# Pooled attention ahead of two gated MLPs: the attention rebuilt around two score products and a maximum inside the product

## The chip, the cores and the metric

The program runs on one NeuronCore of a Trainium2 chip. The metric is device time of one execution in microseconds (us); times of the same kernel agree within about 0.3%.

## The reference

```python
# q, k, v: 2 batches x 8 heads x 1152 tokens x 64, float32
q_pool = q.reshape(B, H, S // 2, 2, D).mean(axis=3)          # 576 pooled queries
scores = (1 / sqrt(D)) * q_pool @ k.transpose(0, 1, 3, 2)     # 576 x 1152 a head
scores = scores - max(scores, axis=-1)
attn = exp(scores); attn = attn / (sum(attn, axis=-1) + 1e-9)
x = (attn @ v) -> 1152 tokens x 512
h = relu(x @ w_in) ** 2;  y = h @ w_out                       # 512 -> 2048 -> 512
out = ((y @ w_a) * (y @ w_b)) @ w_out2                        # 512 -> 1536 -> 512
```

The weights arrive as float64 words; the chip makes float32 of them. A float32 operand x is split into hi, which is x rounded to float32r (12 significant bits), and lo = x - hi; a product is hi*hi + hi*lo + lo*hi.

## The kernel before

Work is done head by head in three stages: the attention (16 heads), then `mlp1`, then `mlp2`; the two MLPs take their products from `split_mm` (L488 to L490). Instructions run on each engine in the order in which the program issues them (a manual schedule). TensorE (PE) is followed in two rows, matmuls and weight loads (PEld).

In the attention a head has two units, each one half of its 576 queries: 288 columns. The steps of a unit u:

- `trans` (L285, L293) transposes [hi | lo] of k and of the pooled q, so that the 128 partitions hold 64 hi and 64 lo features. `kT` is [k_hi; k_lo], `qB` is [q_hi; q_lo], `qC` is the same with its halves exchanged.
- `scores` (L321, L322): for each of the 9 key tiles `kT` is the stationary side, and `qB`, then `qC` move past it, so that all four parts of the product are added up. ScalarE (ACT) copies the result from PSUM to SBUF (L247). Keys lie on partitions, queries along the columns.
- `colmax` (L333): VectorE (DVE) takes the maximum over the 9 key tiles, and GpSimd (POOL) takes it over the 128 partitions with `partition_all_reduce` (L338), result in `gm`.
- `sub` (L342): DVE subtracts `gm`, three key tiles at a time; `expo` (L346): ACT takes the exponential in place.
- `values` (L355): v, with a block of ones beside it for the denominators, is the stationary side; the float32 exponentials, not split, move past it, 9 products of 288 columns.
- `denom`, `recip`, `scale`, `x_hi`, `x_lo` divide by the denominators and write the split result to `xh`, `xl`, which the first MLP reads.

The START table writes out the order of the first units; from then on a fixed pattern of slots has the scores of a unit four slots ahead of its values. POOL also does the splits of k and q (L261, L265, L274), two small transfers for `qC` (L304, L305) and parts of the end. In the last four slots the first four MLP tiles (`early_mm`, `early_post`) and their weights (`w_step`) are worked in.

Of the kernel before, what the change touches and what calls it, by code (L numbers as in the profile page):

```python
# [23 lines left out]
k_hi 0 1 A; q_sum 0 0 V; k_hi 0 0 V; k_hi 0 2 V; k_lo 0 0 P; q_hi 0 0 A; q_lo 0 0 V; q_sum 0 1 V; q_hi 0 1 A  # L24
k_lo 0 1 V; k_lo 0 2 P; trans 0 3 o AAA; q_lo 0 1 P; k_hi 1 * V; trans 0 0 t V; trans 0 1 o A
trans 0 4 o VAV; q_sum 1 * V; q_hi 1 * V; scores 0 0 A; load_q 2; k_lo 1 * P; scores 0 1 A; trans 1 2 o A
load_k 3; trans 0 2 o V; scores 0 2 A; load_k 2; load_v 2; scores 2 0 A; trans 1 1 t A; colmax 0 0
q_lo 1 * P; scores 0 3 A; scores 0 4 A; trans 1 0 t A; load_q 3; q_sum 2 * P; colmax 0 1; trans 1 3 o AVV
q_sum 3 * P; q_hi 2 * V; scores 2 1 A; scores 2 2 A; load_v 3; k_hi 3 * A; scores 2 3 A; k_lo 3 * P
k_hi 2 * V; q_lo 2 * V; load_q 4; trans 1 4 o AAV; k_lo 2 * P; scores 1 0 A; scores 2 4 A; trans 2 4 o AAA  # L30
sub 0 0; scores 1 1 A; scores 3 0 A; load_v 0; colmax 2; trans 2 3 o AAV; w_load 3; load_k 4; scores 1 2 A
trans 3 0 o A; q_hi 3 * V; scores 1 3 A; load_k 5; trans 3 2 o A; q_lo 3 * P; trans 2 2 t A; scores 3 1 A
sub 0 1; q_sum 4 * P; trans 2 0 o V; scores 1 4 A; expo 0 0; scores 3 2 A; sub 0 2; load_q 5; scores 4 0 A
trans 3 1 t A; expo 0 1; values 0 0; colmax 1; sub 2 0; scores 3 3 A; scores 3 4 A; trans 2 1 t A; expo 0 2
trans 3 3 o VVV; values 0 1; trans 3 4 o AAV; w_step 2; scores 4 1 A; values 0 2; k_hi 4 * A; sub 2 1
scores 4 2 A; values 0 3; k_lo 4 * P; expo 2 0; load_v 1; q_hi 4 * A; load_k 6; sub 2 2; values 0 4
q_lo 4 * P; colmax 3; sub 1 0; scores 5 0 A; sub 1 1; q_sum 5 * P; scores 4 3 A; expo 2 1; values 2 0
scores 5 1 A; expo 2 2; load_q 6; scores 5 2 A; values 2 1; scores 4 4 A; values 2 2; denom 0; scores 5 3 A
expo 1 0; scores 5 4 A; k_hi 5 * A; sub 1 2; values 2 3; values 2 4; w_step 2
"""  # L40
START_SLOT = 2


@with_exitstack
def kernel(
# [646 lines left out]
```

## Time and profile before

| | |
|---|---|
| time, median of 2 runs | 985.65 us (985.35 to 985.96) |
| the profiled execution: span | 983.4 us (which of the two times is its own is not listed; the median lies 2.25 us above the span) |
| PE matmuls busy | 729.4 us, 74% |
| DVE busy | 557.4 us, 57% |
| ACT busy | 419.5 us, 43% |
| POOL busy | 151.7 us, 15% |

The span is from the first to the last instruction. A row of a group gives the instructions of one source line with their mean length, then the idle time of their engine just before them and what ended it; "issue" there is time in which the engine waited for nothing that the profile shows. [...] Matmuls are pipelined: what one costs is read from the distance between the starts of two, not from its own length.

### The profile page before, as it was taken

The page shows a single profiled execution, that of the slowest core. Times are in us where ns is not written, and L with a number is a line of the kernel's source. Part 1 is how long each engine was busy: PE and PEld are TensorE (multiplying, and loading weights), DVE is VectorE, ACT ScalarE, POOL GpSimd, SP SyncE. Part 2 cuts the span into 40 slices and gives each one's busy share as a digit, 9 for nine tenths or more (in the row PEclk, how much of TensorE's full clock was granted, in tenths as well). Part 3 has the DMA queues.
Part 4 walks back from the last instruction along what each step waited for, and adds up shares of the span by engine and source line. Part 5 has one row for each costly group of instructions (what it writes and reads, how often), then busy time and mean ns, then how long its engine had stood idle before and what let it go on. Part 6 is the DMA issues. An engine that isn't in the chain of part 4 may idle for free. (4 is left out here: it accounts for less than half of the span.)

```text
span 983.4 us, 10073 instructions
## 1 busy us (share of the span) xinstructions
PE 729.4 (74%) x3830; PEld 659.7 (67%) x3830; DVE 557.4 (57%) x657; ACT 419.5 (43%) x769; POOL 151.7 (15%) x151
## 2 busy tenths in 40 slices
PE   6372757446366366357446899999999999999998
PEld 5362545335345255246335799999999999899987
DVE  7546474544635445455556789349756677127721
ACT  6353535345345344345332656237523454225510
POOL 3211322123123122123111222000000000000000
PEclk9696777867767767778677899999999999999999
DMA  5210502102003003001000122223213333103212
GB/s 151 83 48 1 115 24 49 24 25 58 14 24 73 0 25 72 1 12 37 0 1 0 43 86 87 87 84 108 68 62 105 110 128 117 57 22 116 77 33 65
DMA packets 57905, 56.36 MB, mean 57 GB/s; under 512 B 21024, under 2 KB 50400, under 8 KB 57856
## 3 DMA queue, kind: packets, MB, share of 16 engines
q1 hardware_dynamic: 55712, 51.88, 18.5%
q0 software_dynamic: 1920, 3.54, 1.7%
q8 instruction: 30, 0.49, 0.2%
q10 hardware_dynamic: 224, 0.30, 0.1%
q14 instruction: 19, 0.16, 0.0%
HBM read 49.81 MB, written 2.36 MB: 53 GB/s over the span
## 5 line engine op out<-in xcount | busy, mean ns | idle before, releaser
L333 DVE TENSOR_REDUCE mx<-s 128x288 f32<-128x2592 f32 (+1 forms) x32 | 146.8, 4587 | 235.0 <-POOL gm L338 234.7
L355 PE MATMUL o<-s,v 128*128 128x288 f32 x576 | 192.1, 463 | 8.2 <-ACT s L346 7.6
L321 PE MATMUL ps<-qB,kT 128*128 128x288 f32 x288 | 117.6, 419 | 100.9 <-ACT s L247 100.7
L321 PEld LDWEIGHTS ps<-qB,kT 128*128 128x128 f32 x288 | 63.9, 222 | 112.6 <-ACT s L247 107.6
L355 PEld LDWEIGHTS o<-s,v 128*128 128x128 f32 x576 | 118.2, 222 | 30.4 <-ACT s L346 8.3
L293 PE MATMUL pt<-idr,qhl 96*128 96x96 f32 x96 | 21.4, 348 | 105.6 <-POOL qhl L274 105.0
L346 ACT ACTIVATE s<-s 128x864 f32<-128x864 f32 x96 | 88.5, 924 | 25.1 <-DVE s L342 24.9
L342 DVE TENSOR_TENSOR s<-s,gm 128x864 f32<-128x864 f32 x96 | 96.3, 1057 | 2.6 <-POOL gm L338 2.6
L247 ACT COPY s<-ps 128x576 f32<-128x576 f32 (+1 forms) x160 | 91.6, 585 | 10.5 <-PE ps L322 8.1
L322 PE MATMUL ps<-qC,kT 128*128 128x288 f32 x288 | 92.5, 332 | 1.6 <-DVE qC L249 1.6
L293 PEld LDWEIGHTS pt<-idr,qhl 96*128 96x128 f32 x96 | 14.8, 182 | 116.1 <-POOL qhl L274 110.6
L168 DVE TENSOR_TENSOR wlo<-wx,whi 128x512 fp32r<-128x512 f32 x60 | 41.8, 696 | 54.6 <-ACT whi L134 54.5
L322 PEld LDWEIGHTS ps<-qC,kT 128*128 128x128 f32 x288 | 65.2, 226 | 6.1 <-DVE qC L249 1.8
L338 POOL PARTITION_ALL_REDUCE gm<-mx x32 | 38.5, 1202 | 191.9 <-issue 164.6
L134 ACT CAST whi<-wx 128x512 fp32r<-128x512 f32 x68 | 42.1, 620 | 55.9 <-DVE wx L153 55.8
L489 PE MATMUL y<-gl,whi 128*128 128x384 f32 x192 | 64.6, 337 | 1.2 <-DVE gl L479 1.2
L488 PE MATMUL y<-gh,whi 128*128 128x384 f32 x192 | 64.6, 336 | 0.0
L490 PE MATMUL y<-gh,wlo 128*128 128x384 f32 x192 | 64.6, 336 | 0.0
L247 ACT CAST qB<-pt 128x288 fp32r<-128x288 f32 x30 | 12.0, 401 | 117.2 <-PE pt L293 117.1
L490 PE MATMUL h<-xh,wlo 128*128 128x384 f32 (+1 forms) x176 | 57.6, 327 | 0.0
L488 PE MATMUL h<-xh,whi 128*128 128x384 f32 (+1 forms) x176 | 57.5, 327 | 0.0
L489 PE MATMUL h<-xl,whi 128*128 128x384 f32 (+1 forms) x176 | 57.5, 327 | 0.0
(92 smaller groups left out, 1590.2 us busy)
## 6 DMA issues: line engine op xcount, KB each, us to landing
raw<-in_moe_w_out_dram SPq DMA_DIRECT2D x28, 512.0 KB, 3.3
raw<-in_moe_w_in_dram SPq DMA_DIRECT2D x16, 512.0 KB, 3.8
raw<-in_moe_w_a_dram SPq DMA_DIRECT2D x12, 512.0 KB, 3.5
raw<-in_moe_w_b_dram SPq DMA_DIRECT2D x12, 512.0 KB, 3.5
v<-in_v_dram SPq DMA_DIRECT2D x16, 288.0 KB, 4.2
kin<-in_k_dram SPq DMA_DIRECT2D x15, 288.0 KB, 2.9
qin<-in_q_dram SPq DMA_DIRECT2D x15, 288.0 KB, 3.3
qC<-qB POOLq DMA_DIRECT2D x24, 144.0 KB, 4.3
```

Of the source, the lines that this page charges most:

```text
L134: nc.scalar.copy(w["hi"], w["x"].bitcast(F32))
L168: eng.tensor_tensor(out=lo, in0=x.bitcast(F32), in1=hi.bitcast(F32), op=ALU.subtract)
L247: nc.scalar.copy(out, in_)
L321: nc.tensor.matmul(pt[:, t - 2 * j, :CQ], w, qB[h][:, sl], start=True, stop=False)
L322: nc.tensor.matmul(pt[:, t - 2 * j, :CQ], w, qC[h][:, sl], start=False, stop=True)
L333: nc.vector.tensor_reduce(out=e, in_=st[u][:, kts].rearrange("p c q -> p q c"), op=ALU.max, axis=AX.X)
L342: nc.vector.tensor_tensor(out=s, in0=s, in1=g[:, None, :].to_broadcast([P, 3, CQ]), op=ALU.subtract)
L346: nc.scalar.activation(s[:, 3 * i:3 * i + 3, :], s[:, 3 * i:3 * i + 3, :], AF.Exp, scale=SCALE)
L355: nc.tensor.matmul(om[u][:, :CQ], w, st[u][:, t, :], start=t == 0, stop=t == KT - 1)
L488: nc.tensor.matmul(ps, lh, rh, start=i == 0, stop=False)
L489: nc.tensor.matmul(ps, lh, rl, start=False, stop=False)
L490: nc.tensor.matmul(ps, ll, rh, start=False, stop=i == n - 1)
```

## The change

A head is worked on whole, all 576 queries at once, and the scores are made twice.

First (`maxima`) with 116 queries as the stationary side and the keys moving: queries lie on partitions, so DVE's reduction along the columns (negated) gives each query's maximum over half of the keys; ten such pieces make a head, five groups of queries that start at the columns in `QO` (the last overlaps the one before by 4). `max_split` joins the halves, splits the negated maximum into hi and lo and puts both beside zeros into `mz`; `trans_max` transposes this, so that the negated maximum lies in rows D and D + 1 of `qb`, under the high part of q. `kb` holds the high part of k above rows of ones.

Second (`scores`): `k1` x `qa` and `kb` x `qb` in one accumulation; the rows of ones add the negated maximum, so PSUM holds scores with the maximum subtracted, and ACT takes the exponential straight from PSUM. `exp_hi` (ACT) and `exp_lo` (DVE) split it. In `values` the split exponentials are the stationary side, 116 queries each, and [v_lo | v_hi | 1 1] moves: 130 columns past the high part, 66 past the low one. The result has queries on partitions; `normal` scales it there, and `trans_x` transposes each pair of heads into `xh`, `xl`. Copies that cross partitions (`move`) are transfers on SyncE's (SP's) queue; splits of q, k and v go to POOL. The START table, the warm-up products, `colmax`, `sub`, `denom`, `recip`, `scale` are gone. PSUM has three shared two-bank tiles and one two-bank output tile. The MLPs are not changed; their weights are first requested in the last head.

```diff
-START = """
...
-START_SLOT = 2
...
+    TQ = 116
+    QO = [0, 116, 232, 348, 460]
+    NQ = len(QO)
+    VW = 2 * D + 2
...
-            ps_s = es.enter_context(tc.tile_pool(name="ps_s", bufs=2, space=PSUM))
-            ps_o = es.enter_context(tc.tile_pool(name="ps_o", bufs=3, space=PSUM))
-            ps_t = es.enter_context(tc.tile_pool(name="ps_t", bufs=1, space=PSUM))
...
+            ps_p = es.enter_context(tc.tile_pool(name="ps", bufs=3, space=PSUM))
+            po_p = es.enter_context(tc.tile_pool(name="po", bufs=1, space=PSUM))
...
+            k1 = [ap.tile([P, S], F32R, name=f"k1_{i}") for i in range(NB)]
+            kb = [ap.tile([P, S], F32R, name=f"kb_{i}") for i in range(NB)]
+            qa = [ap.tile([P, SQ], F32R, name=f"qa_{i}") for i in range(NB)]
+            vv = [ap.tile([P, KT, VW], F32R, name=f"vv_{i}") for i in range(NB)]
+            qb = [ap.tile([P, SQ], F32R, name=f"qb_{i}") for i in range(2)]
+            q0 = [pp.tile([P, SQ], F32R, name=f"q0_{i}") for i in range(2)]
+            mz = [pp.tile([TQ, NQ, P], F32R, name=f"mz_{i}") for i in range(2)]
...
+            def move(out, in_):
+                nc.sync.dma_start(out=out.bitcast(F32), in_=in_.bitcast(F32))
...
+                t = k1[h % NB]
+                sl = slice(6 * part * P, (6 * part + n) * P)
+                copy(e, t[:, sl].rearrange("p (b w) -> p b w", b=n // 3), ps[:, :n // 3, :3 * P].bitcast(F32))
+                move(kb[h % NB][:D, sl], t[:D, sl])
...
+                t = qa[h % NB]
+                copy(e, t.rearrange("p (b w) -> p b w", b=2), ps[:, :, :CQ].bitcast(F32))
+                move(q0[h % 2][:D], t[D:])
+                move(t[D:], t[:D])
...
+            def maxima(h, n):
+                i, half = divmod(n, 2)
+                if n == 0:
+                    mh[h] = ap.tile([TQ, NQ, 2], F32, tag="mh", bufs=2, name=f"mh{h}")
+                ps = ps_tile(f"pm{h}_{n}")
+                qs = slice(QO[i], QO[i] + TQ)
+                for c in range(2):
+                    ks = slice((2 * half + c) * CQ, (2 * half + c + 1) * CQ)
+                    nc.tensor.matmul(ps[:TQ, c, :CQ], qa[h % NB][:, qs], k1[h % NB][:, ks], start=True, stop=False)
+                    nc.tensor.matmul(ps[:TQ, c, :CQ], q0[h % 2][:, qs], kb[h % NB][:, ks], start=False, stop=True)
+                nc.vector.tensor_reduce(
+                    out=mh[h][:, i, half:half + 1], in_=ps[:TQ, :, :CQ], op=ALU.max, axis=AX.XY, negate=True
+                )
+            def max_split(h):
+                m = mh.pop(h)
+                z = mz[h % 2]
+                nm = ap.tile([TQ, NQ], F32, tag="nm", bufs=2, name=f"nm{h}")
+                nc.vector.tensor_tensor(out=nm, in0=m[:, :, 0], in1=m[:, :, 1], op=ALU.min)
+                nc.vector.tensor_copy(z[:, :, D], nm)
+                less("V", z[:, :, D + 1], nm, z[:, :, D])
+                move(qb[h % 2][:D], q0[h % 2][:D])
...
+            def trans_max(h, e="A"):
+                ps = ps_tile(f"px{h}", F32R)
+                for i in range(NQ):
+                    nc.tensor.matmul(
+                        ps[:, i // 4, (i % 4) * TQ:(i % 4 + 1) * TQ], mz[h % 2][:, i, :], idr[:TQ, :TQ],
+                        is_transpose=True, start=True, stop=True,
+                    )
+                for sl, src in by_tiles(ps):
+                    copy(e, qb[h % 2][D:, sl], src[D:].bitcast(F32))
...
+            def scores(h, t):
+                ps = ps_tile(f"ps{h}_{t}")
+                ks = slice(t * P, (t + 1) * P)
+                for c in range(2):
                     sl = slice(c * CQ, (c + 1) * CQ)
...
-                copy(e, st[u][:, 2 * j:2 * j + len(kts), :], pt[:, :len(kts), :CQ])
-
...
-                nc.vector.tensor_reduce(out=e, in_=st[u][:, kts].rearrange("p c q -> p q c"), op=ALU.max, axis=AX.X)
...
-                    nc.gpsimd.partition_all_reduce(g, m, P, bass.bass_isa.ReduceOp.max)
...
-            def sub(u, i):
-                s, g = st[u][:, 3 * i:3 * i + 3, :], mx_t[u]
-                nc.vector.tensor_tensor(out=s, in0=s, in1=g[:, None, :].to_broadcast([P, 3, CQ]), op=ALU.subtract)
-
-            def expo(u, i):
-                s = st[u]
-                nc.scalar.activation(s[:, 3 * i:3 * i + 3, :], s[:, 3 * i:3 * i + 3, :], AF.Exp, scale=SCALE)
...
-                    nc.tensor.matmul(om[u][:, :CQ], w, st[u][:, t, :], start=t == 0, stop=t == KT - 1)
...
+                    nc.tensor.matmul(ps[:, c, :CQ], k1[h % NB][:, ks], qa[h % NB][:, sl], start=True, stop=False)
+                    nc.tensor.matmul(ps[:, c, :CQ], kb[h % NB][:, ks], qb[h % 2][:, sl], start=False, stop=True)
+                e = ex[h, t] = ap.tile([P, SQ], F32, tag="ex", bufs=3, name=f"ex{h}_{t}")
+                nc.scalar.activation(e.rearrange("p (b w) -> p b w", b=2), ps[:, :, :CQ], AF.Exp, scale=SCALE)
...
+            def exp_hi(h, t):
+                eh[h, t] = ap.tile([P, SQ], F32R, tag="eh", bufs=4, name=f"eh{h}_{t}")
+                nc.scalar.copy(eh[h, t], ex[h, t])
...
+            def exp_lo(h, t, e="V"):
+                el[h, t] = ap.tile([P, SQ], F32R, tag="el", bufs=4, name=f"el{h}_{t}")
+                less(e, el[h, t], ex.pop((h, t)), eh[h, t])
...
+            def values(h, t):
+                if t == 0:
+                    ou[h] = po_p.tile([P, 2, 512], F32, tag="o", name=f"o{h}")
+                hi, lo = eh.pop((h, t)), el.pop((h, t))
+                for i in range(NQ):
+                    b, c0 = i // 3, (i % 3) * VW
+                    qs = slice(QO[i], QO[i] + TQ)
+                    o = ou[h][:TQ, b]
+                    nc.tensor.matmul(
+                        o[:, c0:c0 + VW], hi[:, qs], vv[h % NB][:, t, :],
+                        start=t == 0 and i % 3 == 0, stop=t == KT - 1, skip_group_check=True,
+                    )
+                    nc.tensor.matmul(
+                        o[:, c0 + D:c0 + VW], lo[:, qs], vv[h % NB][:, t, D:],
+                        start=False, stop=t == KT - 1, skip_group_check=True,
+                    )
...
+            def normal(h):
...
+                for sl, src in parts:
+                    nc.scalar.copy(ol[:, sl], src[:, :, :D])
+                for sl, src in parts:
+                    nc.vector.tensor_scalar(out=dn[:, sl], in0=src[:, :, 2 * D], scalar1=1e-9, scalar2=None, op0=ALU.add)
+                for sl, src in parts:
+                    nc.vector.tensor_tensor(out=ol[:, sl], in0=src[:, :, D:2 * D], in1=ol[:, sl], op=ALU.add)
+                nc.vector.reciprocal(dn, dn)
+                x = xt[h // 2][:, :, (h % 2) * D:(h % 2 + 1) * D]
+                nc.gpsimd.tensor_tensor(out=x, in0=ol, in1=dn[:, :, None].to_broadcast([TQ, NQ, D]), op=ALU.mult)
...
+            def trans_x(p):
...
+                for sl, src in by_tiles(ps):
+                    to = slice(b * SQ + sl.start, b * SQ + sl.stop)
+                    nc.scalar.copy(xh[:, pr, to], src)
+                    less("V", xl[:, pr, to], src, xh[:, pr, to])
...
+            split_q(0, "VAV")
+            split_k(0, "AV")
+            load(2)
+            trans_q(0)
+            trans_k(0, 0)
+            trans_k(0, 1)
...
+            for n in range(2 * NQ):
+                maxima(0, n)
+                if n == 2:
...
+            max_split(0)
...
+            trans_max(0)
+            MAXIMA = (2, 1, 1, 2, 1, 1, 2, 0, 0)
...
+            for h in range(NH + 1):
+                n = 0
+                for t in range(KT if h < NH else 2):
+                    if h < NH:
+                        scores(h, t)
+                        exp_hi(h, t)
+                    if h + 1 < NH:
+                        for _ in range(MAXIMA[t]):
+                            maxima(h + 1, n)
+                            n += 1
+                    if h < NH:
+                        exp_lo(h, t)
+                    g = h * KT + t - 2
+                    if g >= 0:
+                        values(*divmod(g, KT))
+                    if t == 1 and h:
+                        normal(h - 1)
...
+                    if h + 2 < NH:
+                        if t == 1:
+                            trans_k(h + 2, 0)
+                        if t == 2:
+                            trans_k(h + 2, 1)
+                        if t == 4:
+                            trans_q(h + 2)
+                    if t == 5 and h and h % 2 == 0:
+                        trans_x(h // 2 - 1)
+                    if h + 1 < NH:
+                        if t == 7:
+                            max_split(h + 1)
+                        if t == 8:
+                            trans_max(h + 1)
+                    if t == 2 and h + 3 < NH:
+                        split_k(h + 3)
+                    if t == 4 and h + 3 < NH:
+                        split_q(h + 3)
+                        load(h + 4)
+                    if t == 5 and h + 2 < NH:
+                        split_v(h + 2)
+                        load_v(h + 4)
+                    if h == NH - 1:
                         w_step(NE)
-                if s - 1 in do_t:
-                    load_v(do_t[s - 1])
-                if s == NU - 5:
-                    qk_stack.close()
+                        w_step(NE)
+                        if t in (2, 4, 6, 8):
+                            early_mm(ps_p, t // 2 - 1)
+                        if t in (3, 5, 7):
+                            early_post(gpool, t // 2 - 1)
+                if h == NH - 2:
+                    prep_stack.close()
                     gpool = gs.enter_context(tc.tile_pool(name="gpool", bufs=1, side="right", reuse_waits="tile"))
+            early_post(gpool, 3)
+            trans_x(NH // 2 - 1)
```

POOL, from the split of a head on, in the kernel before (`gm` is the maximum over partitions, `khl` and `qhl` the split k and q; an ISA row without tiles changes POOL's configuration):

```order
L338 ISA
L338 ISA gm_898<-mx_896 128x288
L261 ISA
L261 TENSOR_TENSOR khl_894<-kin_616,khl_894 128x9x64
L274 TENSOR_TENSOR qhl_923<-qin_619,qhl_923 96x6x64
L304 DMA qC_917<-qB_916 64x576
L305 DMA qC_917<-qB_916 64x576
L392 TENSOR_TENSOR xl<-xf_563,xh 128x288
L338 ISA
L338 ISA gm_988<-mx_986 128x288
```

And in the changed kernel, one whole head (`xt` the scaled output, `vv` the split v):

```order
L397 TENSOR_TENSOR xt_1272<-ol_1587,dn_1588 116x5x64
L237 CAST khl_1640<-kin_1403 128x9x64
L244 TENSOR_TENSOR khl_1640<-kin_1403,khl_1640 128x9x64
L251 TENSOR_TENSOR qin_1405<-qin_1405 96x6x64
L237 CAST qhl_1713<-qin_1405 96x6x64
L244 TENSOR_TENSOR qhl_1713<-qin_1405,qhl_1713 96x6x64
L237 CAST vv_108<-vin_1121 128x9x64
L244 TENSOR_TENSOR vv_108<-vin_1121,vv_108 128x9x64
```

The maximum and every change of configuration have left POOL; the casts of k, q and v and the low part of v have come to it.

PE in the middle of the attention before (`o` the output, `s` the exponentials, `v` values and ones):

```order
L321 MATMUL ps_0_2274<-qB_2112,kT_2111 128x288
L322 MATMUL ps_0_2274<-qC_2113,kT_2111 128x288
L321 MATMUL ps_0_2274<-qB_2112,kT_2111 128x288
L322 MATMUL ps_0_2274<-qC_2113,kT_2111 128x288
L355 MATMUL o_2280<-s_1981,v_92 128x288 x2
```

And one step of the changed kernel, a key tile t of a head: its scores (`ps`), a piece of the next head's maxima (`pm`), and the values (`o`) of the key tile two steps back, of whose five pairs of products two are shown:

```order
L347 MATMUL ps_4_3279<-qa_105,k_0_99 128x288
L348 MATMUL ps_4_3279<-qb_112,kb_102 128x288
L347 MATMUL ps_4_3279<-qa_105,k_0_99 128x288
L348 MATMUL ps_4_3279<-qb_112,kb_102 128x288
L310 MATMUL pm_6_3288<-k_1_100,qa_106 116x288
L311 MATMUL pm_6_3288<-kb_103,q_0_113 116x288
L310 MATMUL pm_6_3288<-k_1_100,qa_106 116x288
L311 MATMUL pm_6_3288<-kb_103,q_0_113 116x288
L368 MATMUL o_3226<-vv_108,eh_2_3216 116x130
L372 MATMUL o_3226<-vv_108,el_2_3224 116x66
L368 MATMUL o_3226<-vv_108,eh_2_3216 116x130
L372 MATMUL o_3226<-vv_108,el_2_3224 116x66
```

The value products have become ten narrow ones a key tile, and the products for the maxima stand between the scores and them.

PE of the changed kernel where one head's steps end and the next one's begin (`px` the transposed maxima, which ACT copies into `qb`):

```order
L368 MATMUL o_3226<-vv_108,eh_6_3362 116x130
L372 MATMUL o_3226<-vv_108,el_6_3376 116x66
L332 MATMUL px_3435<-idr,mz_115 128x116 x5
L347 MATMUL ps_0_3443<-qa_106,k_1_100 128x288
L348 MATMUL ps_0_3443<-qb_111,kb_103 128x288
```

The second product of the new head reads `qb`, which hangs on the transposition two rows above it.

## Rows read from the trace of the kernel before

**Rows 1.** The page: the span, busy time by engine, the granted clock in 40 slices.

```profile
span 983.4 us, 10073 instructions
...
PE 729.4 (74%) x3830; PEld 659.7 (67%) x3830; DVE 557.4 (57%) x657; ACT 419.5 (43%) x769; POOL 151.7 (15%) x151
...
PEclk9696777867767767778677899999999999999999
```

**Rows 2.** Stretches: busy us (instructions) of each engine, granted clock, DMA share, GB/s.

```profile
383.00:393.00 10.00, 9.63 (x55) 7.76 (x53) 7.17 (x4) 7.30 (x13) 2.30 (x3) 1.00 0.27 59
440.00:560.00 120.00, 71.61 (x320) 58.94 (x321) 72.15 (x53) 48.04 (x80) 22.10 (x23) 0.79 0.07 18
566.00:983.40 417.40, 411.88 (x2312) 399.36 (x2310) 246.90 (x446) 168.59 (x324) 13.63 (x10) 1.00 0.27 83
```

**Rows 3.** The page's costliest groups: busy us, mean ns, idle before them.

```profile
L333 DVE TENSOR_REDUCE mx<-s 128x288 f32<-128x2592 f32 (+1 forms) x32 | 146.8, 4587 | 235.0 <-POOL gm L338 234.7
...
L338 POOL PARTITION_ALL_REDUCE gm<-mx x32 | 38.5, 1202 | 191.9 <-issue 164.6
```

**Rows 4.** The line of the maximum over partitions: its instructions, min/median/max ns.

```profile
L338 POOLq MODIFY_POOL_CONFIG  x62: 1/4/49, 14.0 to 542.6; - x62
```

**Rows 5.** Timeline: start us, length us, instruction, idle before it and what ended it.

```profile
260.48 4.50 DVE L333 TENSOR_REDUCE mx<-s 128x288 f32<-128x2592 f32 x1 [8.04 <-POOL gm L338]
...
271.76 0.61 PE L321 MATMUL ps<-qB,kT 128*128 128x288 f32 x1 [14.73 <-ACT s L247]
...
276.76 4.57 DVE L333 TENSOR_REDUCE mx<-s 128x288 f32<-128x2592 f32 x1 [7.02 <-POOL gm L338]
```

**Rows 6.** Timeline of PE: products of 288 columns, and the f32 value products.

```profile
388.50 1.14 PE L355 MATMUL o<-s,v 128*128 128x288 f32 x4
389.25 0.51 PE L321 MATMUL ps<-qB,kT 128*128 128x288 f32 x1
389.60 0.29 PE L322 MATMUL ps<-qC,kT 128*128 128x288 f32 x1
...
565.98 0.30 PE L488 MATMUL h<-xh,whi 128*128 128x288 f32 x1
...
573.10 0.29 PE L488 MATMUL h<-xh,whi 128*128 128x288 f32 x1
```

**Rows 7.** Timeline of PE: transpositions, 288 columns at the low clock, 256 columns.

```profile
10.65 0.63 PE L285 MATMUL pt<-idr,khl 128*128 128x128 f32 x6
11.21 0.40 PE L321 MATMUL ps<-qB,kT 128*128 128x288 f32 x1
...
531.00 0.45 PE L488 MATMUL e<-xh,whi 128*128 128x288 f32 x1
531.24 0.45 PE L489 MATMUL e<-xl,whi 128*128 128x288 f32 x1
...
977.97 0.28 PE L489 MATMUL o<-wlo,th 128*128 128x256 f32 x1
978.09 0.28 PE L490 MATMUL o<-whi,tl 128*128 128x256 f32 x1
```

**Rows 8.** Groups by line, each shape apart: busy us, mean ns, idle before.

```profile
L247 ACT COPY s<-ps 128x576 f32<-128x576 f32 x128 | 79.4, 631 | 5.4 <-PE ps L322 3.3
...
L261 POOL TENSOR_TENSOR khl<-kin,khl 128x576 fp32r<-128x576 f32 x15 | 26.9, 1798 | 84.4 <-issue 77.4 <-ACT s L346 7.0
...
L247 ACT CAST khl<-kin 128x576 fp32r<-128x576 f32 x13 | 8.8, 675 | 0.1
...
L479 DVE TENSOR_TENSOR gl<-g,gh 128x576 fp32r<-128x576 f32 x4 | 3.5, 865 | 0.4
...
L333 DVE TENSOR_REDUCE mx_end<-s 128x288 f32<-128x864 f32 x1 | 1.1, 1130 | 0.0
```

**Rows 9.** The page's DMA issues: count, KB each, median us from issue to landing.

```profile
raw<-in_moe_w_in_dram SPq DMA_DIRECT2D x16, 512.0 KB, 3.8
...
qC<-qB POOLq DMA_DIRECT2D x24, 144.0 KB, 4.3
```

**Rows 10.** Timeline of PE: the first scores.

```profile
9.39 0.37 PE L321 MATMUL ps<-qB,kT 128*128 128x288 f32 x1 [0.24 <-DVE kT L249]
```

More of the change, by code (lines that the diff above doesn't have):

```diff
@@ L18 @@
 PSUM = bass.MemoryType.PSUM
-START = """
[L24 to L40, printed above, removed]
-START_SLOT = 2
 @with_exitstack
@@ L243, in attention @@
+            for i in range(2):
+                nc.gpsimd.memset(q0[i][D:].bitcast(F32), 0.0)
+                nc.gpsimd.memset(mz[i].bitcast(F32), 0.0)
             engines = {"A": nc.scalar, "V": nc.vector, "P": nc.gpsimd}
@@ L249, in copy @@
                     engines[e].tensor_copy(out, in_)
-            def part(c):
-                return slice(None) if c == "*" else slice(3 * int(c), 3 * int(c) + 3)
-            def k_hi(h, c="*", e="A"):
-                if h not in khl:
-                    khl[h] = qk.tile([P, KT, 2, D], F32R, tag="khl", bufs=2, name=f"khl{h}")
-                copy(e, khl[h][:, part(c), 0, :], kin[h][:, part(c)])
-            def k_lo(h, c="*", e="P"):
-                hi, lo = (khl[h][:, part(c), i, :] for i in range(2))
-                engines[e].tensor_tensor(out=lo, in0=kin[h][:, part(c)], in1=hi.bitcast(F32), op=ALU.subtract)
@@ L263, in q_sum @@
-            def q_sum(h, c="*", e="P"):
-                a, b = (qin[h][:, part(c), i, :] for i in range(2))
-                engines[e].tensor_tensor(out=a, in0=a, in1=b, op=ALU.add)
-            def q_hi(h, c="*", e="A"):
-                if h not in qhl:
-                    qhl[h] = qk.tile([QP, QT, 2, D], F32R, tag="qhl", bufs=2, name=f"qhl{h}")
-                copy(e, qhl[h][:, part(c), 0, :], qin[h][:, part(c), 0, :])
-            def q_lo(h, c="*", e="P"):
-                hi, lo = (qhl[h][:, part(c), i, :] for i in range(2))
-                engines[e].tensor_tensor(out=lo, in0=qin[h][:, part(c), 0, :], in1=hi.bitcast(F32), op=ALU.subtract)
@@ L398, in attention @@
-            load_k(1)
-            load_q(1)
-            warm = ps_t.tile([P, 512], F32R, tag="t", name="warm")
-            for i in range(NWARM):
-                nc.tensor.matmul(warm[:, :P], idr, idr, is_transpose=True, start=True, stop=True)
-            steps = dict(
-                load_k=load_k, load_q=load_q, load_v=load_v, k_hi=k_hi, k_lo=k_lo, q_sum=q_sum, q_hi=q_hi, q_lo=q_lo,
-                trans=trans, scores=scores, colmax=colmax, sub=sub, expo=expo, values=values, denom=denom,
-                w_load=w_load, w_step=w_step,
-            )
@@ L408, in attention @@
-            for step in START.replace("\n", ";").split(";"):
-                if step.strip():
-                    name, *args = step.split()
-                    steps[name](*(int(a) if a.isdigit() else a for a in args))
-            do_a, do_b, do_t = {}, {}, {}
-            for h in range(2, NH):
-                t = 4 * (h // 2) - 6 + h % 2 + (h < 4)
-                do_t[t], do_b[t - 1], do_a[t - 2] = h, h, h
-            seq = [0, 2, 1, 3] + list(range(4, NU))
-            def at_slot(f, p, *args, second=False):
-                if 0 <= p < NU and not (second and unit(seq[p])[2] == 0):
-                    f(seq[p], *args)
```

265 lines of the change are left out of this document (100 added, 165 removed).

## The prediction

> **What bounds the kernel now.** I read the page first: TensorE (PE) is 74% busy, but its slices fall into two stages, with half-idle digits and a granted clock of 0.6 to 0.8 up to slice 22, and 9s at full clock behind it [rows 1]. The stretches put the border in time: from 566.0 us, when the first product belonging to the MLP alone starts, PE is busy 411.9 of 417.4 us at clock 1.00, while 440 to 560 us shows 71.6 busy of 120 at 0.79 [rows 2]. The change touches the first stage; the 417.4 us behind it keep their instructions, and I carry them over whole.
>
> Inside the attention no engine is full, so the question is which wait ends last. The groups by line name it: VectorE (DVE) waits 234.7 us in front of its column maximum, all for `gm`, the maximum over partitions that GpSimd (POOL) makes [rows 3]. POOL's own idle time shows why: it sits before `gm` 164.6 us on "issue", that is, on nothing that the profile shows, and 77.4 us before the split of k [rows 3, 8]; 62 changes of the POOL configuration stand on the line of the maximum [rows 4]. The maximum itself takes 1.2 us; what costs is POOL's change between it and ordinary arithmetic, some 5 us each way (164.6 over 32 maxima, 77.4 over 15 splits). The timeline shows the beat: column maxima start at 260.48 and 276.76 us, one half-head (a unit) in 16.3 us, and the second comes behind 7.02 us of idle DVE [rows 5]. 32 such units make the 566 us.
>
> **The change, part by part.** Removed: all 32 partition maxima, their configuration changes, 96 subtractions on DVE and the plain-f32 value products. The listing of POOL's new order holds no configuration change between heads, so this bound goes entirely. What is late next is read by adding up each engine for one head (16 heads).
>
> PE. Products of 288 columns: from 565.98 to 573.10 us 54 of them start one behind the other at full clock, 0.132 us each [rows 6]; I take 0.133. Scores: 9 key tiles x 4 = 36, 4.8 us. Maxima: 10 x 4 = 40, 5.3 us. Values: 9 tiles x 5 query groups = 45 pairs, one product of 130 moving columns and one of 66, each with a new stationary of 116 columns. No row has a float32r product this narrow, so I bound it. Below: 288 columns cost 0.133 and 256 cost 0.12 [rows 6, 7], 0.41 ns a column; a pair is (130 + 66) x 0.41 = 0.08 us, and 0.11 with the 15 ns that each product has left over. Above: the f32 values of now, where four records and one product of 0.133 fill 388.50 to 389.60, so 0.24 a record; 576 records for 288 value products make two each, 0.48 us for 288 columns or 1.68 ns a column [rows 6]; a pair is then 0.33. The nearest row in width and type is the transposition of 128 float32r columns with a new 128-column stationary each: six in 0.56 us, 0.093 [rows 7]. I take 0.09 a product, 0.18 a pair, 8.1 us a head. [...] Transpositions: 9 for k, 6 for q, 5 for the maxima and half of 5 for the output (plain f32, taken double), 2.2 us. Sum for PE 20.4 us.
>
> ScalarE (ACT): 9 exponentials over 128x576 from PSUM at the copy's 0.63, 9 casts at 0.675 [rows 8], some 2,900 columns of other copies at the copy's 1.1 ns: 15.0 us. DVE: 9 differences at 0.865 [rows 8] and 10 maxima over 576 columns, between 1.31 ns a column (1.13 us for 864) and the strided 1.77 (4.59 us for 2592) [rows 3, 8], so 7.5 to 10.2, with 1.5 for the rest 16.8 to 19.5 us. POOL: four passes over 128x576 at 1.8 [rows 8], three over 96x384 at about two thirds of it, one scaling: some 12 us. None reaches PE's 20.4; PE sets the beat, and these are paid by nothing as long as they stay in step.
>
> PE's waits. At the end of a head the maxima are transposed, ACT copies them behind one exponential and one cast (1.3 + 0.6 us), and the next head's second product waits for that: about 2 us, of which nothing covers more than the first product. Two steps later the first value product waits until `normal` has read the single output tile: ACT 0.4, DVE 0.8, partly beneath transpositions, scores and maxima: about 1 us. One more for single lateness in the three shared PSUM tiles. I take 4 us a head, bounds 0 and 8. Sum 24.4 us a head against 2 x 16.3 now. The eight transfers of a head on SP's queue (two for k, two for q, one for the query part of `qb`, three loads) run a head ahead of their readers; the nearest transfers of now, halves of q between partitions, land in 4.3 us [rows 9], so I cost them at nothing; if that lead is gone they stand in PE's wait.
>
> Start. Now the first scores start at 9.39 us [rows 10] from loads cut in pieces on two queues and a written-out order. The new start loads whole heads on one queue (3 us more), needs two moves of q one after the other (6 us), ten maxima at DVE's 0.9 us (9 us) and the transposed maximum (2.5 us): 30 us, bounds 22 and 40.
>
> Last head. No maxima: 4.8 + 8.1 + 4 of waits, plus the four early MLP tiles, 96 x 0.133 = 12.8 us, plus one wait of ACT for the first raw weights, which are only now requested, 3.8 us [rows 9]: 33.5 us. Behind it two value steps, normalizing and the last transposition: 6 us.
>
> Sum: 30 + 15 x 24.4 + 33.5 + 6 = 435.5 us in place of 566.0, a gain of 130.5. The span of 983.4 becomes 852.9. The median of the runs, 985.65, lies 2.25 us above this span, which I add: **855 us**.
>
> **The rivals.** B: narrow float32r products run at the f32 rate, 0.33 us a pair. For it: every float32r product in the trace that isn't a transposition has 256 columns or more, so nothing shows the fast rate below; against it: the price still falls from 288 to 256 columns, and the transpositions are fast. A head gains 6.7 us of PE and loses about 1 of waits: 30.1 us; 36 + 15 x 30.1 + 39 = 527 us, so 947 us in all, 930 to 985 with the other bounds.
>
> C: waits of 8 us a head in place of 4, since PE, ACT and DVE hand each tile on in strict order and only three PSUM tiles serve scores, maxima and transpositions: 15.5 x 4 = 62 us more, 917 us.
>
> D, on the other side: PE falls to its low clock. The same 288 columns take 0.24 us at 531 us [rows 7]; a head whole at that level is 76 x 0.24 + 16.2 + 4.4 + 4 = 42.8 us, and the kernel about 1158. It becomes slower than before by 2% once about half of the attention's PE work runs low (150 of the 303 us); with 70% it is 1067 us. For it: the attention of now runs at 0.79, and narrow products keep the array less busy. Against it: the low stretches of now come behind waits like the 14.73 us before 271.76, and the dense 383 to 393 us, with 9.6 busy of 10, has 1.00 [rows 2, 5]; the new waits are a few us at most.
>
> **How the numbers follow.** The forecast (8 to 11 us of waits and price either way, 815 to 905) gets 0.54, B 0.25, C 0.09, D 0.12. Faster by over 2% (below 966; 2% is about what a measurement of this kernel tells from no change) are the forecast, C and most of B (0.18): 0.81. Within 2%: the upper part of B (0.06) and 0.01 of D: 0.07. Slower: 0.11 of D and 0.01 of B: 0.12. The range 815 to 970 leaves out D, about 0.04 of B above and 0.04 of the forecast below.
>
> **What would show it.** The first `h` product near 436 us. In a steady head: POOL without waits on "issue"; value products of 130 and 66 columns starting 0.18 us a pair apart (B: about 0.33); PE busy over 80% at a clock near 1.0 (D: below 0.75); DVE's reductions at 0.75 to 1.0 us; PE's only long wait at the head's change, for ACT's copy into `qb`, near 2 us. I am wrong if PE waits in every step for ACT or DVE (C), if a step waits for a transfer, or if the stretch behind the attention no longer takes 417 us.

## The result, and the profile after

The changed kernel takes **846.25 us**, median of 2 runs (841.21 and 851.28), against 985.65: a ratio of 0.8597 [0.8467, 0.8728]. Forecast: 855, range 815 to 970. Two later series of the same kernel gave 0.8657 [0.8608, 0.8705] and 0.8619 [0.8596, 0.8642]. Its twelve executions lie between 841.21 and 856.77 us, wider than the 0.3% named at the start, and the longer ones have the lower mean clock (that granted to TensorE, as a share of its full clock): 0.983 in the shortest, 0.966 in the longest.

The page of the kernel after: the span, busy time by engine, the clock in 40 slices, two groups of DVE and the exponential, answering to [rows 1, 3].

```profile
span 839.4 us, 13712 instructions
PE 790.3 (94%) x5422; PEld 768.9 (92%) x5422; DVE 514.4 (61%) x920; ACT 424.6 (51%) x758; POOL 145.3 (17%) x143
PEclk9899999999999999997999999999999999999999
L312 DVE TENSOR_REDUCE mh<-pm 116x1 f32<-116x576 f32 x160 | 117.5, 755 | 87.7 <-PE pm L311 87.7
L350 ACT ACTIVATE ex<-ps 128x576 f32<-128x576 f32 x144 | 93.9, 652 | 95.7 <-PE ps L348 70.0
L244 DVE TENSOR_TENSOR el<-ex,eh 128x576 fp32r<-128x576 f32 x144 | 112.4, 781 | 47.9 <-ACT eh L354 43.3
```

PE is the busiest engine, as forecast, at 94%: DVE and ACT stand idle mostly for its products. That its own waits are close behind as a bound, experiments 4 and 5 show. The one group of POOL that stood behind a change of configuration (the split of k) now has no wait to speak of; the columns are busy us, mean ns, idle before:

```profile
L244 POOL TENSOR_TENSOR khl<-kin,khl 128x576 fp32r<-128x576 f32 x15 | 27.0, 1799 | 1.1
```

Stretches of the kernel after (columns as in [rows 2]): the steady heads, the last head's middle, and the part behind the attention.

```profile
53.00:380.00 327.00, 307.73 (x2625) 301.44 (x2624) 219.09 (x392) 211.75 (x361) 105.82 (x100) 0.99 0.25 66
380.00:400.00 20.00, 15.74 (x102) 15.06 (x101) 9.79 (x20) 10.00 (x18) 1.07 (x1) 0.74 0.18 54
421.50:839.40 417.90, 414.39 (x2313) 402.20 (x2311) 244.38 (x444) 168.44 (x322) 11.65 (x8) 1.00 0.27 83
```

The first `h` product starts at 421.52 us (forecast 436) and the rest takes the 417.9 us that I had carried over. The whole gain lies in the attention.

PE's timeline after, four places: the first transposed maxima, a run of value products, one head's change, and value products in the last head with the transposed maxima ahead of them.

```profile
26.52 0.81 PE L332 MATMUL px<-idr,mz 116*128 116x116 f32 x5 [1.84 <-DVE mz L244]
...
148.64 0.30 PE L368 MATMUL o<-vv,eh 128*116 128x130 f32 x1
148.77 0.23 PE L372 MATMUL o<-vv,el 128*116 128x66 f32 x1
148.84 0.30 PE L368 MATMUL o<-vv,eh 128*116 128x130 f32 x1
148.98 0.23 PE L372 MATMUL o<-vv,el 128*116 128x66 f32 x1
149.04 0.30 PE L368 MATMUL o<-vv,eh 128*116 128x130 f32 x1
...
212.20 0.59 PE L332 MATMUL px<-idr,mz 116*128 116x116 f32 x5 [0.31 <-DVE mz L244]
...
214.00 0.37 PE L348 MATMUL ps<-qb,kb 128*128 128x288 f32 x1 [1.01 <-DMA qb<-q]
...
378.31 0.60 PE L332 MATMUL px<-idr,mz 116*128 116x116 f32 x5 [0.31 <-DVE mz L244]
...
385.90 0.43 PE L368 MATMUL o<-vv,eh 128*116 128x130 f32 x1
386.14 0.34 PE L372 MATMUL o<-vv,el 128*116 128x66 f32 x1
386.29 0.43 PE L368 MATMUL o<-vv,eh 128*116 128x130 f32 x1
```

A pair of value products costs 0.20 us (148.64, 148.84, 149.04; clock 1.00 in 148 to 150 us), and 0.39 at the low clock (385.90 to 386.29; 0.50 in 385.5 to 387 us). At the head's change PE waits 0.3 us for the maxima and 1.0 for the transfer that brings the query part into `qb`. `px` (the transposed maxima) starts at 26.5 us for head 0 and at 378.3 for head 15: 23.45 us a head, forecast 24.4.

### The profile page after: what moved, and what is told of

The parts are those of the page before. It is cut to its first block, busy times and chain, and to the rows that moved or that the text cites. A ratio compares the mean times of both kernels' runs of the same rounds, so it can differ in the third digit from the quotient of the medians.

```text
span 839.4 us, 13712 instructions
## 1 busy us (share of the span) xinstructions
PE 790.3 (94%) x5422; PEld 768.9 (92%) x5422; DVE 514.4 (61%) x920; ACT 424.6 (51%) x758; POOL 145.3 (17%) x143
## 4 chain that ended last, share of the span: by engine, by line
PE 80%; ACT 5%; DMA 4%; DVE 4%; issue 4%; POOL 2%; SPq 1%; POOLq 0%; DVEq 0%; ACTq 0%
PE o L368 7%; PE pm L310 4%; PE o L372 4%; PE y L508 4%; PE y L509 4%; PE y L510 4%; PE pm L311 4%; PE ps L348 4%; PE ps L347 4%; PE h L508 4%; PE h L509 4%; PE h L510 4%; PE a L510 3%; PE b L510 3%; PE a L509 3%
## 5 line engine op out<-in xcount | busy, mean ns | idle before, releaser
L312 DVE TENSOR_REDUCE mh<-pm 116x1 f32<-116x576 f32 x160 | 117.5, 755 | 87.7 <-PE pm L311 87.7
L368 PE MATMUL o<-vv,eh 128*116 128x130 f32 x720 | 151.6, 285 | 2.6 <-DVE dn L395 2.6
L372 PE MATMUL o<-vv,el 128*116 128x66 f32 x720 | 151.9, 236 | 0.0
L350 ACT ACTIVATE ex<-ps 128x576 f32<-128x576 f32 x144 | 93.9, 652 | 95.7 <-PE ps L348 70.0
L244 DVE TENSOR_TENSOR el<-ex,eh 128x576 fp32r<-128x576 f32 x144 | 112.4, 781 | 47.9 <-ACT eh L354 43.3
L368 PEld LDWEIGHTS o<-vv,eh 128*116 128x116 f32 x720 | 131.6, 183 | 3.6 <-issue 3.0
L372 PEld LDWEIGHTS o<-vv,el 128*116 128x116 f32 x720 | 131.6, 183 | 0.0
L310 PE MATMUL pm<-k,qa 128*116 128x288 f32 x320 | 92.7, 307 | 12.3 <-DVE xl L244 6.5
L354 ACT CAST eh<-ex 128x576 fp32r<-128x576 f32 x144 | 96.9, 673 | 4.6
L347 PE MATMUL ps<-qa,k 128*128 128x288 f32 x288 | 93.3, 337 | 0.0
```

The costliest lines, as they stand in the source:

```text
L244: engines[e].tensor_tensor(out=out, in0=x, in1=hi.bitcast(F32), op=ALU.subtract)
L310: nc.tensor.matmul(ps[:TQ, c, :CQ], qa[h % NB][:, qs], k1[h % NB][:, ks], start=True, stop=False)
L312: nc.vector.tensor_reduce(out=mh[h][:, i, half:half + 1], in_=ps[:TQ, :, :CQ], op=ALU.max, axis=AX.XY, negate=True)
L347: nc.tensor.matmul(ps[:, c, :CQ], k1[h % NB][:, ks], qa[h % NB][:, sl], start=True, stop=False)
L354: nc.scalar.copy(eh[h, t], ex[h, t])
L368: nc.tensor.matmul(o[:, c0:c0 + VW], hi[:, qs], vv[h % NB][:, t, :], start=t == 0 and i % 3 == 0, stop=t == KT - 1, skip_group_check=True,)
```

## The experiments

The theory: before, the maximum on POOL cost a change of configuration each way, and taking POOL's other work from it frees the attention whatever else is rebuilt; after, PE's own work sets the beat. Rivals: the rebuilding itself made the gain (fewer DVE passes, split products); and, for what is left, waits rather than PE's work.

**1. The change again**, unchanged, timed twice more beside the kernel before.

> The changed kernel as it stands, timed again beside the kernel before: 841 to 851 us if its two first times show its spread. If the spread comes from stretches at the low clock, the execution with the lower mean clock is the longer one.

Measured 851.33 us (847.25 to 856.77; 0.977 of full clock in the fastest, 0.966 in the slowest). The second series, **after_base**:

> The changed kernel once more, as the base for the runs beside it: 845 to 857 us, the longer executions at the lower mean clock.

849.35 us (844.65 to 851.47). One hundredth of mean clock goes with 8 to 9 us, so differences under some 5 us are read together with the clock.

**2. The old kernel, with POOL left to the maximum alone.** Nothing rebuilt; 14 letters in START and these lines:

```diff
-            def k_lo(h, c="*", e="P"):
+            def k_lo(h, c="*", e="V"):
...
-                nc.gpsimd.tensor_tensor(out=x[0:D], in0=x[0:D], in1=r[0:D], op=ALU.mult)
+                nc.vector.tensor_tensor(out=x[0:D], in0=x[0:D], in1=r[0:D], op=ALU.mult)
...
-                eng = nc.vector if u == NU - 1 else nc.gpsimd
+                eng = nc.vector
```

(`q_sum`, `q_lo` and `w_stage` likewise.)

> The kernel before with one edit: every split, sum and scaling that GpSimd made goes to VectorE; the maximum over partitions stays on GpSimd, so its configuration is not changed between heads. Theory 1 (the changes of configuration bounded the kernel before): the beat of a unit falls from 16.3 us to VectorE's sum, 4.6 + 3.2 + 1.0 + about 2 for the moved work = 10.8 to 12 us, so 32 units take 345 to 385 us and the kernel 790 to 830 us. Rival (the maximum over partitions itself is slow, and its 1.2 us in the trace are only its visible part): the beat stays near 16 us and the kernel near 985 us, or above it for the work that VectorE takes over.

**791.17 us**, 0.8036 [0.8018, 0.8055]: faster than the whole rebuild. Its line of the maximum, its column maxima on the timeline, and a stretch of its steady part:

```profile
L338 POOLq MODIFY_POOL_CONFIG  x2: 1/1/1, 12.8 to 12.8; - x2
```

```profile
162.44 4.78 DVE L333 TENSOR_REDUCE mx<-s 128x288 f32<-128x2592 f32 x1 [0.58 <-POOL gm L338]
...
172.22 4.78 DVE L333 TENSOR_REDUCE mx<-s 128x288 f32<-128x2592 f32 x1
```

```profile
60.00:340.00 280.00, 226.31 (x1142) 178.74 (x1140) 274.92 (x199) 195.27 (x351) 115.35 (x52) 0.93 0.21 49
```

2 changes of configuration instead of 62 [rows 4], a unit in 9.8 us instead of 16.3 [rows 5], and DVE, which had waited 235 us for `gm` [rows 3], busy 274.92 of 280 us. The edit takes POOL's ordinary work away together with the changes, but that work and the maximum kept POOL busy for 22.10 of 120 us only [rows 2], 3 us a unit. So the bound was the changes of configuration; experiment 3 puts them back without a reader.

**3. The change, with two maxima a head put back on POOL**, their result unused.

```diff
+            dead = pp.tile([P, 2, CQ], F32, name="dead")
+            nc.gpsimd.memset(dead, 0.0)
+            def dead_max():
+                nc.gpsimd.partition_all_reduce(dead[:, 1], dead[:, 0], P, bass.bass_isa.ReduceOp.max)
...
+                        dead_max()
                         split_q(h + 3)
...
+                        dead_max()
```

> The changed kernel with two maxima over partitions a head put back on GpSimd, before and behind the split of q, on constant data and with nobody reading their result: 4 changes of configuration a head in 13 heads. Theory 1 (the changes cost about 5 us each, whoever reads the result): GpSimd needs 7.7 + 2 x 3.8 + 4 x 5 = 35 us a head, more than the beat of 23.4, so it becomes the bound, 13 x 12 = 150 us more, near 1000 us. Rival (only a result that is waited for costs): no change, near 850 us.

1170.33 us, 1.1883 [1.1818, 1.1947]; the direction as expected, the size not. POOL's timeline, then PE's longest wait in 100 to 600 us and SP's for POOL in the whole execution (us in total, times, longest):

```profile
299.68 1.17 POOL L381 PARTITION_ALL_REDUCE dead<-dead  x1 [5.81 <-issue]
307.81 1.52 POOL L251 TENSOR_TENSOR qin<-qin 96x384 f32<-96x384 f32 x1 [6.96 <-issue]
...
317.69 1.17 POOL L381 PARTITION_ALL_REDUCE dead<-dead  x1 [6.23 <-issue]
318.75 0.74 POOL L237 CAST vv<-vin 128x576 fp32r<-128x576 f32 x1
326.57 1.30 POOL L244 TENSOR_TENSOR vv<-vin,vv 128x576 fp32r<-128x576 f32 x1 [7.08 <-issue]
```

```profile
PE ps L348 <- DMA qb<-q: 226.3, 10, 26.8
...
SPq L209 <- POOL vv L244: 302.3, 14, 27.1
```

POOL idles 6 to 7 us at each change, four times a head, 26 us. The way to the maximum shows 5.81 and 6.23 us, the way back 6.96 and 7.08. On the way back the idle time stands before the next TENSOR_TENSOR: the cast of v between them (318.75) starts at once. Nobody reads `dead`, and yet PE waits up to 26.8 us a head: the transfer into `qb` stands on SP's queue behind a load of v (L209), which waits until POOL has split the v before it. I had expected PE to be touched far less; what is queued behind the late engine's readers decided.

**4. What a pair of value products costs.** Three edits of `values` (L368 to L375), each on its own: hi moves 66 columns for 8 of 9 key tiles (**hi66**), lo has 64 stationary columns in place of 116 (**lo_stat64**), lo moves 130 columns (**lo130**).

```diff
+                    c1 = 0 if t == 0 else D
...
-                        o[:, c0:c0 + VW], hi[:, qs], vv[h % NB][:, t, :],
+                        o[:, c0 + c1:c0 + VW], hi[:, qs], vv[h % NB][:, t, c1:],
```

```diff
-                        o[:, c0 + D:c0 + VW], lo[:, qs], vv[h % NB][:, t, D:],
+                        o[:64, c0 + D:c0 + VW], lo[:, QO[i]:QO[i] + 64], vv[h % NB][:, t, D:],
```

```diff
-                        o[:, c0 + D:c0 + VW], lo[:, qs], vv[h % NB][:, t, D:],
+                        o[:, c0:c0 + VW], lo[:, qs], vv[h % NB][:, t, :],
```

> The changed kernel, but the high exponentials' product moves 66 columns in place of 130 in eight of nine key tiles (it leaves out the low part of v there). Theory W (a value product costs what loading its 116 stationary columns takes, 0.10 us): no change, within 0.5%. Rival C (it costs its moving columns): 640 products lose 64 columns at 0.41 ns, 17 us less.

> The changed kernel, but the product of the low exponentials has 64 stationary columns in place of 116 (it leaves out the low part for 52 of 116 queries); its 66 moving columns stay. Theory W (weight load, about 0.86 ns a stationary column): 720 products lose 52 columns each, 0.045 us, so 32 us less, about 812 us, if TensorE still sets the beat; a pair then starts every 0.155 us. Rival C (moving columns, or a fixed floor for each product): no change.

> The changed kernel, but the low exponentials' product moves all 130 columns in place of 66 (the low part of v is multiplied too). Theory W (a value product costs its weight load): a pair still starts every 0.20 us; and if the clock falls where TensorE spends its time on loading stationary columns with few moving ones, the mean clock rises above the base's 0.97 and the kernel gets some us faster, 838 to 850 us. Rival C (moving columns are paid): 720 products gain 64 columns at 0.41 ns, 19 us more.

PE's timeline of hi66, of lo_stat64 and of lo130:

```profile
149.83 0.27 PE L369 MATMUL o<-vv,eh 128*116 128x66 f32 x1
149.93 0.27 PE L373 MATMUL o<-vv,el 128*116 128x66 f32 x1
150.03 0.27 PE L369 MATMUL o<-vv,eh 128*116 128x66 f32 x1
```

```profile
146.56 0.29 PE L368 MATMUL o<-vv,eh 128*116 128x130 f32 x1
146.69 0.20 PE L372 MATMUL o<-vv,el 128*64 128x66 f32 x1
146.72 0.30 PE L368 MATMUL o<-vv,eh 128*116 128x130 f32 x1
```

```profile
148.56 0.27 PE L372 MATMUL o<-vv,el 128*116 128x130 f32 x1
148.66 0.27 PE L368 MATMUL o<-vv,eh 128*116 128x130 f32 x1
148.76 0.26 PE L372 MATMUL o<-vv,el 128*116 128x130 f32 x1
```

66, 98 or 130 moving columns a product on average: 0.20 us a pair each time. Fewer stationary columns, 116 and 64: 0.16. At these widths the price follows the stationary columns, not the moving ones. The times followed it only in part: lo_stat64 gave 841.66 us (0.8538 [0.8487, 0.8589]), 8 to 10 less than the change where 32 had been expected. The distances give it 45 x 0.04 = 1.8 us a head; the rest went to PE's waits, above all those at the head's change (idle in 100 to 340 us: 22.0 us, in the change 14.1), and to the clock. lo130 gave 846.12 us (0.8587 [0.8565, 0.861]), no slower than after_base with more columns to move, at a clock of 0.979 to 0.987 against 0.971 to 0.979. hi66 scattered with its clock, from 853.48 us at 0.965 to 884.56 at 0.928, so only its distances are used here.

**5. Less work for PE:** the maxima from one product in place of two.

```diff
-                    nc.tensor.matmul(ps[:TQ, c, :CQ], qa[h % NB][:, qs], k1[h % NB][:, ks], start=True, stop=False)
-                    nc.tensor.matmul(ps[:TQ, c, :CQ], q0[h % 2][:, qs], kb[h % NB][:, ks], start=False, stop=True)
+                    nc.tensor.matmul(ps[:TQ, c, :CQ], qa[h % NB][:, qs], k1[h % NB][:, ks], start=True, stop=True)
```

> The changed kernel, but each piece of the maxima is made with one product, k times the high part of q, without the low part of q (a softmax is the same for any subtracted number near the maximum). 320 products of 288 columns go, 0.133 us each. Theory PE (TensorE sets the beat of 23.4 us a head): 2.65 us a head, 40 us in all, less what the waits for ScalarE and VectorE give back; with lo_stat64's 0.8 to 1 us gained a head out of 1.8 as a guide, 20 to 40 us, so 810 to 830 us. Rival E (ScalarE and VectorE already end the waits): under 10 us. If fewer moving columns cost clock, the mean clock falls below 0.97 and the gain with it.

866.79 us in the median, 0.8777 [0.8743, 0.8811], from 847.28 us at a clock of 0.939 to 878.93 at 0.891. The fastest execution, the one profiled, lies 2.6 us above after_base's fastest: 20 products fewer a head (2.7 us by 0.133, 40 in all) gained nothing. Its steady stretch; then one head's change, with the transfer into `qb` leaving SP, PE's wait for it, and the ten us that follow:

```profile
100.00:370.00 270.00, 246.22 (x1936) 240.30 (x1934) 190.26 (x321) 174.49 (x299) 87.70 (x83) 0.90 0.27 71
```

```profile
122.64 0.47 SPq L241 DMA_DIRECT2D qb<-q  x1
...
127.33 0.52 PE L347 MATMUL ps<-qb,kb 128*128 128x288 f32 x1 [1.81 <-issue]
```

```profile
127.50:137.50 10.00, 10.00 (x50) 10.00 (x51) 4.99 (x11) 4.98 (x9) 1.40 (x3) 0.50 0.03 7
```

The clock is 0.90 where the kernel after has 0.99. In 100 to 370 us it falls five times, always in or directly behind PE's wait for this transfer at a head's change (1.3 to 2.3 us each). The profile calls four of these waits "issue", but each ends 0.1 us after the transfer has landed. With less work ahead of it PE comes to the head's change sooner than the transfer, which SP issues only behind the moves and loads of other heads. The kernel after has the same wait at up to 1.3 us and two falls.

As an estimate, the longer idle time (23.8 us of 270, in the kernel after 15.2) takes 0.8 us a head, and the low clock (with the 0.50 of 127.5 to 137.5 us as the low level, 0.90 is 54 of 270 us at it; a product there takes 0.24 us for 0.133) 1.9 more than in the kernel after: together the 2.7 saved. So PE's work is not the whole bound after: two cuts of it, in experiment 4 and here, went for the most part into waits and clock. No run moved this transfer by itself; that is untested.

Now hi66, an execution of 880.45 us, behind a wait for the same transfer:

```profile
56.35 0.58 PE L348 MATMUL ps<-qb,kb 128*128 128x288 f32 x1 [1.55 <-DMA qb<-q]
```

```profile
60.00:75.00 15.00, 15.00 (x83) 15.00 (x84) 7.69 (x14) 6.18 (x11) 7.64 (x8) 0.58 0.09 22
```

The clock, at 1.00 up to 55 us, falls in this wait and stays low until 72.6 us, though PE shows no idle time after 56.35. Why it stayed low through 15.00 of 15 busy us, the profile's busy time does not show. Nor does each short wait bring a fall: 0.4 us at a head's change did in hi66 (229.9 us; 0.89 in 225 to 240 us) and did not in the kernel after (144.9 us; 1.00 in 145 to 150 us). What else decides isn't settled by these runs.

**6. Fewer, wider value products:** v stationary again, as [v_hi | 1] and [v_lo | 0], with the split exponentials moving: 54 products of 288 columns a head instead of 45 pairs, and no transposition of the output.

```diff
...
+                w = vv[h % 2]
+                for b in range(2):
+                    o, qs = ou[h][:, b, :CQ], slice(b * CQ, (b + 1) * CQ)
+                    nc.tensor.matmul(o, w[:, t, :P], hi[:, qs], start=t == 0, stop=False, skip_group_check=True)
+                    nc.tensor.matmul(o, w[:, t, P:], hi[:, qs], start=False, stop=False, skip_group_check=True)
+                    nc.tensor.matmul(o, w[:, t, :P], lo[:, qs], start=False, stop=t == KT - 1, skip_group_check=True)
...
```

> The changed kernel with the sides of the value products exchanged back: [v_high | ones] and [v_low | zeros] are the stationary side, and the split exponentials move, 3 x 2 products of 288 columns a key tile in place of 10 narrow ones; the division goes back to half-heads on all 128 partitions, the transposition of the output is gone. Maxima, scores and splits stay. Theory W: 54 x 0.133 = 7.2 us a head in place of 45 x 0.205 = 9.2, and 0.45 less of transpositions, 2.4 us a head or 37 in all; and since every product but the transpositions moves 288 columns, the mean clock of the attention rises to 0.99, some 8 us more: 800 to 815 us. Rival E (ScalarE's and VectorE's turns end the waits, as lo_stat64 gave back only half): 830 us. Rival C (narrow products were no dearer than their columns): 9 x 196 x 5 columns are fewer than 54 x 288, so slower than 850 us.

A miss: 867.7 us, 0.8808 [0.8782, 0.8833]. Only rival C's figure fits, and its reason was refuted in experiment 4. PE at a head's change, and a stretch:

```profile
206.38 0.84 PE L336 MATMUL px<-idr,mz 116*128 116x116 f32 x5 [3.52 <-DVE mz L247]
...
209.69 0.44 PE L314 MATMUL pm<-k,qa 128*116 128x288 f32 x1
209.93 0.44 PE L315 MATMUL pm<-kb,q 128*116 128x288 f32 x1
```

```profile
100.00:320.00 220.00, 189.01 (x1267) 179.56 (x1265) 151.16 (x195) 134.31 (x219) 83.05 (x72) 0.89 0.25 64
```

PE now reaches the head's change before the maxima are split and waits 3.52 us in every second head, since `max_split` is issued on DVE behind the low half of key tile 7, which waits for ACT. Behind the wait 288 columns take 0.24 us: the low clock (0.72 in 204 to 216 us). With one product for the maxima as well (**v_stat_max_one**, the edit of 5):

> v_stat with the maxima made by one product each, as in max_one. If max_one gained nothing because the clock fell (narrow value products then being a larger share of TensorE's time), the same cut among wide products keeps the clock at 0.97 or more and gains 20 to 40 us against v_stat: 765 to 790 us. Rival (the cut costs clock whatever stands beside it, or the maxima are no bound): within 10 us of v_stat.

845.14 us, 0.8582 [0.8564, 0.86]: 22.6 less than v_stat, the gain that was expected, but far from the 765 to 790 us, which had been reckoned before v_stat's result; the clock stayed where it was (0.943 to 0.953) in place of 0.97. So I moved the late step: `max_split` from behind key tile 7 to right behind the last maxima of tile 6, `trans_max` from 8 to 7 (**v_stat_early**).

```diff
+                        if t == 6:
+                            max_split(h + 1)
...
                         if t == 7:
-                            max_split(h + 1)
-                        if t == 8:
                             trans_max(h + 1)
```

> The split of the maxima stands ahead of the low half of the exponential of key tile 6 instead of behind that of tile 7, and the transposition of the maxima one key tile earlier. The theory: v_stat lost what its shorter products gave to the wait of 3.5 us for the maxima at each head's change, and to the low clock behind that wait. Then the wait is under 1 us, the mean clock 0.97 or more, and 15 heads x 2.5 to 5 us are saved: 790 to 830 us. The rival: the wait only moves to another place at the head's change, or the clock stays near 0.95 with TensorE fuller: 855 us or more.

830.67 us, 0.843 [0.8391, 0.8468], 37 less than v_stat, just above the upper edge of what the theory gave. The wait for the maxima and the low clock went together:

```profile
189.84 0.59 PE L336 MATMUL px<-idr,mz 116*128 116x116 f32 x5 [0.96 <-DVE mz L247]
...
190.88 0.29 PE L371 MATMUL o<-eh,vv 128*128 128x288 f32 x1
191.02 0.29 PE L372 MATMUL o<-eh,vv 128*128 128x288 f32 x1
```

```profile
100.00:320.00 220.00, 199.15 (x1462) 190.83 (x1463) 167.38 (x222) 153.51 (x248) 90.58 (x78) 0.98 0.27 70
```

The rival was right in part: some of the wait moved to the transfer into `qb`, 16.3 us in this stretch (v_stat 4.8), up to 2.9 us a head.

**7. The version that beats both:** kernel 2, where DVE is full, with the column maximum (strided, 4.78 us) made as eight `tensor_tensor` maxima of 288 columns.

```diff
-                nc.vector.tensor_reduce(out=e, in_=st[u][:, kts].rearrange("p c q -> p q c"), op=ALU.max, axis=AX.X)
+                s, t0, t1 = st[u], kts.start or 0, kts.stop or KT
+                nc.vector.tensor_tensor(out=e, in0=s[:, t0], in1=s[:, t0 + 1], op=ALU.max)
+                for t in range(t0 + 2, t1):
+                    nc.vector.tensor_tensor(out=e, in0=e, in1=s[:, t], op=ALU.max)
```

> old_pool_max_only with VectorE's strided maximum over 9 key tiles (4.78 us a unit) made as a chain of 8 maxima over 288 columns that lie together (0.46 us each, 3.7 us). VectorE was busy 98% of the steady stretch there, 9.8 us a unit. Theory: 1.1 us a unit less, 35 us in all, 756 us. Rival (ScalarE at 70% or TensorE at 81% end the waits next): half of it, 775 us.

**766.88 us** (766.54 to 767.15), 0.7784 [0.777, 0.7799], between the two expectations. DVE's timeline and a stretch:

```profile
158.98 0.44 DVE L334 TENSOR_TENSOR mx<-s 128x288 f32<-128x288 f32 x1
159.45 3.41 DVE L336 TENSOR_TENSOR mx<-mx,s 128x288 f32<-128x288 f32 x7
```

```profile
100.00:320.00 220.00, 182.34 (x957) 145.14 (x958) 211.93 (x332) 164.21 (x296) 50.84 (x43) 0.96 0.20 49
```

DVE's maximum takes 3.9 us instead of 4.8; DVE is still the bound, 96% busy. POOL's maximum became shorter as well, from a median of 3.8 us to 1.8; why is not shown.

## Why the prediction was right, point by point

- **The cause before**: right. Experiments 2 and 3 show it from both sides. I had put a change at some 5 us, 164.6 over 32 maxima; the idle time stood in 27 of them, 6.1 each, and experiment 3 shows 6 to 7. What I did not ask is how much of the gain needs the rebuild: none. In its place the rebuild leaves PE the busiest, at 23.45 us a head, where the old head without the changes takes 2 x 9.8.
- **PE's price of a value pair**: the mis-sized term. I put 0.18 us; it is 0.20, so 9.2 us a head instead of 8.1. I had read six transpositions in 0.56 us [rows 7], but the product behind them, whose weights were loaded behind theirs, starts its next neighbour 0.24 us later instead of 0.13 (11.21 to 11.45 us; clock 1.00 in 10.4 to 11.9 us); with that 0.11 the six took 0.667, 0.111 each. The runs show a price that follows the stationary columns: 0.20 with 116 and 116, 0.16 with 116 and 64 (lo_stat64); at the low clock the first is 0.39. Rival B's 0.33 is refuted.
- **Waits of 4 us a head**: too many. In the steady stretch PE idles 327 - 307.73 = 19.3 us in 13.9 heads, 1.4 a head. 20.4 + 1.1 + 1.4 = 22.9 of the 23.45 us. The transpositions were priced from the same six: at 0.111 the 2.2 us are 2.8, which leaves next to nothing. The errors in price and in waits have opposite signs, so the sum came out closer than its terms; that is luck.
- **The transfers at nothing**: not quite. The one into `qb` does not run a head ahead of its reader; it lands as PE comes for it, and PE waits for it in some heads (1.0 us at 214.00). That was small here, and by the estimate of experiment 5 it is what took back the gain of max_one.
- **Start**: 27.1 us (first scores at 27.12), forecast 30. **Last head and tail**: 378.7 to 421.5, 42.8 us, forecast 39.5, with 0.74 of full clock in 380 to 400 us, which I had not put in.
- Together: -2.9 - 15 x 0.95 + 3.3 = -13.9, from 435.5 to 421.6 us; measured 421.52.
- **D, the low clock**: did not decide here (0.99 in the steady heads). My argument against it named what the falls stand behind, waits, and the wrong size: waits of a few us at most were to be harmless, yet the clock fell behind 1.3 to 2.3 us at a head's change in max_one (0.90 in 100 to 370 us), and twice behind 1.0 to 1.3 in the kernel after (0.73 in 215 to 220 us, 0.71 in 260 to 265). C's waits of 8 us a head did not come.

## What to carry to other kernels

When an engine idles on "issue" beside a special instruction, first move the ordinary work off that engine: here that alone gave 0.80 and one more local edit 0.78, where rebuilding the stage gave 0.86. Before a narrow product is made narrower, price its stationary columns, not only its moving ones (here a pair cost 0.20 us with 66, 98 or 130 columns moving, and 0.16 with fewer stationary); and after any cut of PE's work read its waits where one head hands over to the next, and the granted clock behind them, since a cut of 40 us was taken back there. In a strict order, ask of each step that the next head waits for what stands ahead of it on its engine and on its transfer queue.
